# One ring of eight PSUM banks for all of a fused attention and feed-forward kernel, with its transposes spread

## Chip, cores and metric

One core of a Trainium2 chip. The metric is the device time of one execution in microseconds (us); every kernel that has a ratio ran beside runs of the kernel before on the same chip, and kernels of different calls (partly on different chips) are compared by these ratios. "TensorE" (PE in the profile) multiplies, "VectorE" (DVE) and "ScalarE" (ACT) read its results out of PSUM, "GpSimd" (POOL) casts and masks in SBUF, SP issues most transfers.

## The reference, cut to what matters

```python
# q, k, v: 8 batches x 8 heads x 576 x 64;  s: 8 x 8 x 576
scores = q @ k.T / 8 + min(-(cum_i - cum_j), 0)      # cum: running sum of max(s, 0)
attn = softmax(where(causal, -1e9, scores)) @ v
x = attn.transpose(0, 2, 1, 3).reshape(4608, 512)
out = (silu(x @ w_gate) * (x @ w_val)) @ w_out       # 512 -> 1536 -> 512
```

## The kernel before

Heads go one after the other. The first batch (8 heads) runs alone, since the feed-forward part needs its output; after that, feed-forward units of the tokens that are ready are laid between pieces of attention of the next batch. A unit is 4 matmuls of 512 columns into one PSUM bank: `pg` (gate), `pv` (value) or a third of `py` (output). k and q of a half-batch (4 heads) are transposed, by TensorE for half-batches 0 to 4, by transfers after that. Four extra rows per head in each of k and q (`aug`) carry the bias.

PSUM has 8 banks. They are shared out in three pools:

```python
scp = pool("scp", bufs=3, PSUM)    # scores
avp = pool("avp", bufs=1, PSUM)    # attn @ v
mp  = pool("mp",  bufs=4, PSUM)    # feed-forward, transposes of k and q (tps), of x (xps)
...
def score_piece(bh, ci):           # 4 pieces a head: 512, 512, 512 and 64 columns
    sc = scp.tile([128, 512], FP32, tag="sc")
    # ... one to four matmuls into sc ...
    nc.scalar.activation(pt[...], sc[:, 0:o], AF.Exp, scale=0.125)
    # pieces 0 and 3: GpSimd masks pt
...
def ffn_items(tt):
    for ft in range(12):
        pg = mp.tile(...)          # 4 matmuls
        # ACT: th = tanh(pg / 2);  DVE: pp = (th + 1) * pg
        yield
        pv = mp.tile(...)          # 4 matmuls
        # DVE: ht = pp * pv
        yield
    # ... 4 x py: 12 matmuls, ACT copies, SP stores ...
```

The transposes of half-batches 2 to 4 stand in one block right ahead of the scores that need them:

```python
if not first and step == 0 and 2 <= h < NPE:
    # ...
    cast_one(h, "k", nc.gpsimd); cast_one(h, "q", nc.gpsimd)
    for g in range(2):
        for nm in ("k", "q"):
            pe_transpose(h, nm, g)              # 5 or 4 transposes into one bank
            pe_out(h, nm, g, 0, nc.vector)      # copies partitions 0-63 out
            pe_out(h, nm, g, 1, nc.scalar)      # copies partitions 64-127 out
            yield ...
```

The softmax here doesn't subtract the row's maximum and nothing guards it: scores larger than these inputs give would overflow.

Of the kernel before, what the change touches and what calls it, by code (L numbers as in the profile page):

```python
# [15 lines left out]
ALU = mybir.AluOpType  # L16
# [3 lines left out]
def kernel(  # L20
# [32 lines left out]
    DIAG_OFF = [1088, 1216, 1344, 1472, 1024]  # L53
    OFF_OFF = {0: 0, 3: 448, 1: 512, 2: 832}
# [7 lines left out]
    CHUNK_PT = [1088, 0, 512, 1024]  # L62
# [15 lines left out]
    scp = ctx.enter_context(tc.tile_pool(name="scp", bufs=3, space=PSUM))  # L78
    avp = ctx.enter_context(tc.tile_pool(name="avp", bufs=1, space=PSUM))
    mp = ctx.enter_context(tc.tile_pool(name="mp", bufs=4, space=PSUM))  # L80
# [4 lines left out]
    NPE = 5  # L85
    KS = {i: dram.tile([NR * S, 128], BF16, name=f"ks{i}") for i in range(NPE, NHB)}
# [14 lines left out]
    HL = const.tile([BH, 4, 2, S], BF16)  # L101
    warm = const.tile([128, 1], FP32)

    with tc.manual_schedule():
        loaded = {}
        SRC = {"k": (k, 0), "q": (q, 1)}
# [31 lines left out]
        nc.sync.dma_start(s_sb, s.rearrange("b h n -> (b h) n"))  # L138
        load_qk(0)
        load_qk(1)  # L140
        load_v(0, range(5))

# [7 lines left out]
        nc.vector.memset(warm, 0.0)  # L150
        nc.scalar.activation(warm, warm, AF.Exp)
        nc.vector.memset(one_s, 1.0)
        nc.vector.memset(HL[:, 2:4, 0, :].bitcast(FP32), NEGS2)
        nc.vector.memset(HL[:, 0:2, 1, :].bitcast(FP32), ONES2)
        make_identity(nc, ident)
        for e in range(2):
            nc.gpsimd.memset(aug_rows(0, e)[:, 1, :], ONES2)
            nc.gpsimd.memset(aug_rows(0, e)[:, 0, :], 0.0)

            nc.scalar.copy(  # L160
                KQ[1][e][64 * (1 - e) : 64 * (1 - e) + 64, 1, :],
                one_s[:, 0:1].to_broadcast([64, NR * S + 64]),
            )
        nc.vector.memset(aug_rows(1, 0)[:, 0, :], 0.0)

        nc.vector.tensor_scalar(s_sb, s_sb, 0.0, 8.0, ALU.max, ALU.mult)
        nc.vector.tensor_tensor_scan(c8, one_s, s_sb, 0.0, ALU.mult, ALU.add)  # L167
        nc.vector.tensor_copy(HL[:, 0, 0, :], c8)
        nc.vector.tensor_sub(HL[:, 1, 0, :], c8, HL[:, 0, 0, :])
        nc.vector.tensor_copy(HL[:, 2:4, 1, :], HL[:, 0:2, 0, :])  # L170
        for r in range(2):
            for i in range(2):
                nc.vector.memset(KQ[i][r][64 * r : 64 * r + 64, :, NR * S :], 0.0)

        def aug(hb, engs):
            for hh in range(HB):
                r, e = divmod(hh, 2)
                r0 = 64 * (1 - r)
                engs[hh].dma_start(
                    KQ[hb % 2][r][r0 : r0 + 4, :, e * S : (e + 1) * S],  # L180
                    HL[hb * HB + hh : hb * HB + hh + 1, :, :, :],
                )

# [36 lines left out]
        def pe_transpose(hb, name, g):  # L220
            j0, j1 = JG[g]
            ps = mp.tile([128, j1 - j0, 128], BF16, tag="m", name="tps")
# [5 lines left out]
            tps[name, g] = ps  # L228

        def pe_out(hb, name, g, r, eng):  # L230
# [5 lines left out]
            srcp = tps[name, g][64 * r : 64 * r + 64].rearrange("a j x -> a x j")  # L236
            if eng is nc.scalar:
                nc.scalar.copy(dst, srcp)
            else:
                eng.tensor_copy(dst, srcp)  # L240

# [15 lines left out]

        def score_piece(bh, ci):
            hb, hh = divmod(bh, HB)
            if ci == 0:  # L260
# [4 lines left out]
            sc = scp.tile([128, 512], FP32, tag="sc", name="sc")  # L265
            o = 0
            for (tj, lo, hi) in CHUNKS[ci]:
# [3 lines left out]
                    T[:, 0, e * S + 128 * tj : e * S + 128 * (tj + 1)],  # L271
                    T[:, 1, e * S + lo : e * S + hi],
# [300 lines left out]
```

## Time and profile before

| | before |
|---|---|
| time, median of 4 runs | 414.9 us (413.6 to 415.5) |
| span of the profiled run | 411.9 us |
| TensorE busy | 383.5 us, 93% |
| TensorE busy from 100 to 300 us | 200.0 of 200 us |
| first feed-forward unit starts at | 36.3 us |

A profile line of a group has start or total, duration, engine, source line, operation, output, inputs and count; a bracket gives the idle time of the engine just before and what ended it. In a line of waits the waiting engine and line stand left of the arrow, the one waited for right of it, then total us, times and longest us. In a table of stages, the stretch comes first, then its length and the busy time of PE, PE's weight loads, DVE, ACT and POOL (instructions in brackets), TensorE's granted clock, the share of the DMA engines' time that was busy, and GB/s.

### The profile page before, as it was taken

What the parts mean: (1) busy time and instruction counts of PE and PEld (TensorE: products, weight loads), DVE (VectorE), ACT (ScalarE), POOL (GpSimd) and SP (SyncE); (2) the same over time, 40 slices, a digit from 0 to 9 for tenths busy, and PEclk for the clock granted to TensorE, in tenths of its full rate; (3) what the DMA queues carried; (4) which work ended last, traced back from release to release, by engine and by line L of the source; (5) the groups of instructions that cost most, each with busy time, mean ns of one, the idle gap of its engine ahead of it and who ended that gap; (6) DMA issues with size and microseconds to landing.
All of it is one profiled execution on the core that took longest, in us unless ns stands there. A gap on an engine that the chain in (4) does not pass through costs nothing.

```text
span 411.9 us, 7992 instructions
## 1 busy us (share of the span) xinstructions
PE 383.5 (93%) x3082; PEld 211.9 (51%) x3082; DVE 251.0 (61%) x494; ACT 212.0 (51%) x421; POOL 125.2 (30%) x224
## 2 busy tenths in 40 slices
PE   2687797989999999999999999999999999999996
PEld 1464454645555555555555555555555544444442
DVE  7846666366873588358844884479446733752750
ACT  7463665666555555456545564565556532322321
POOL 4783252743262316131623162316211110000000
PEclk9989998999999999999999999999999999999999
DMA  7999998466845793469346924681410002002002
GB/s 265 146 230 221 268 245 266 122 193 164 210 109 173 179 228 94 148 199 245 81 132 207 260 81 108 216 175 51 116 57 2 2 27 76 0 10 95 0 4 100
DMA packets 85335, 56.71 MB, mean 138 GB/s; under 512 B 65552, under 2 KB 69584, under 8 KB 85296
## 3 DMA queue, kind: packets, MB, share of 16 engines
q1 hardware_dynamic: 81360, 51.40, 44.8%
q0 software_dynamic: 3936, 4.79, 6.9%
q8 instruction: 24, 0.39, 0.4%
q14 instruction: 15, 0.12, 0.1%
HBM read 37.90 MB, written 15.93 MB: 131 GB/s over the span
## 4 chain that ended last, share of the span: by engine, by line
PE 90%; DVE 4%; DMA 2%; ACT 1%; POOL 1%; issue 1%; ACTq 0%; POOLq 0%
PE pg L457 23%; PE py L481 23%; PE pv L470 22%; PE sc L269 11%; PE av L305 7%; PE xps L337 3%; DVE kq L240 2%; DMA kq<-HL 1%; ACT pt L277 1%; DMA s_sb<-in_s_dram 1%; POOL vt L136 1%; PE tps L225 1%; DVE ot L321 1%; DVE c L167 0%; PE avm L305 0%
## 5 line engine op out<-in xcount | busy, mean ns | idle before, releaser
L277 ACT ACTIVATE pt<-sc 128x512 bf16<-128x512 f32 (+1 forms) x256 | 117.7, 505 | 56.2 <-PE sc L269 54.8
L464 DVE SCALAR_TENSOR_TENSOR pp<-th,pg 128x512 bf16<-128x512 bf16 x108 | 74.1, 686 | 63.8 <-ACT th L462 63.4
L457 PE MATMUL pg<-xt,wg 128*128 128x512 bf16 x432 | 111.8, 381 | 0.0
L470 PE MATMUL pv<-xt,wv 128*128 128x512 bf16 x432 | 110.9, 379 | 0.0
L462 ACT ACTIVATE th<-pg 128x512 bf16<-128x512 f32 x108 | 64.5, 597 | 86.0 <-PE pg L457 86.0
L481 PE MATMUL py<-wo,ht 128*128 128x512 bf16 x432 | 105.7, 379 | 0.0
L269 PE MATMUL sc<-kq 128*128 128x128 bf16 (+4 forms) x576 | 76.4, 247 | 10.4 <-DVE kq L240 5.5
L281 POOL TENSOR_SCALAR_AFFINE_SELECT pt<-pt 128x512 bf16<-128x512 bf16 x64 | 40.8, 637 | 140.0 <-ACT pt L277 137.7
L475 DVE TENSOR_TENSOR ht<-pp,pv 128x512 bf16<-128x512 bf16 x108 | 73.9, 684 | 7.9
L269 PEld LDWEIGHTS <-kq 128*128 128x128 bf16 x576 | 46.9, 101 | 44.3 <-issue 7.0
L457 PEld LDWEIGHTS <-wg 128*128 128x128 bf16 x432 | 38.5, 98 | 36.3 <-issue 0.8
L470 PEld LDWEIGHTS <-wv 128*128 128x128 bf16 x432 | 38.4, 98 | 34.8
L481 PEld LDWEIGHTS <-ht 128*128 128x128 bf16 x432 | 38.2, 98 | 34.9
L305 PEld LDWEIGHTS <-pt 128*128 128x128 bf16 x960 | 41.2, 98 | 20.9 <-issue 3.0
L305 PE MATMUL av<-vt,pt 128*128 128x65 bf16 x900 | 47.4, 194 | 2.0 <-POOL vt L136 0.9
L489 ACT ACTIVATE ysb<-py 128x512 f32<-128x512 f32 x36 | 21.5, 598 | 43.6 <-PE py L481 42.4
L286 POOL TENSOR_SCALAR_AFFINE_SELECT pt<-pt 128x64 bf16<-128x64 bf16 x64 | 15.4, 240 | 64.5 <-ACT pt L277 64.4
L341 DVE COPY xt<-xps 128x64 bf16<-128x64 bf16 (+7 forms) x32 | 9.7, 304 | 34.7 <-PE xps L337 34.7
L321 DVE TENSOR_TENSOR ot<-av,rc 128x320 bf16<-128x320 f32 x60 | 29.5, 491 | 2.1
L320 DVE RECIPROCAL rc<-av 128x5 f32<-128x5 f32 x60 | 11.4, 189 | 31.3 <-PE av L305 31.2
L136 POOL CAST vt<-rawv 128x512 bf16<-128x512 f32 (+1 forms) x40 | 25.7, 673 | 0.0
L240 DVE COPY kq<-tps 64x640 bf16<-64x640 bf16 (+1 forms) x24 | 17.5, 762 | 2.3 <-PE tps L225 2.1
(47 smaller groups left out, 160.6 us busy)
## 6 DMA issues: line engine op xcount, KB each, us to landing
rawk<-in_k_dram SPq DMA_DIRECT2D x16, 576.0 KB
rawq<-in_q_dram SPq DMA_DIRECT2D x16, 576.0 KB
out_dram<-ysb SPq DMA_DIRECT2D x36, 256.0 KB
rawv<-in_v_dram SPq DMA_DIRECT2D x32, 256.0 KB
ks<-ck SPq DMA_DIRECT2D x11, 288.0 KB
qs<-cq SPq DMA_DIRECT2D x11, 288.0 KB
wg<-in_moe_w_gate_dram POOLq DMA_DIRECT2D x2, 768.0 KB, 8.8
wv<-in_moe_w_val_dram POOLq DMA_DIRECT2D x2, 768.0 KB, 10.1
```

Of the source, the lines that this page charges most:

```text
L136: eng.tensor_copy(VT[b % 2][0:n, c, :, 0:D], loaded["v", b][0:n, c, :, :])
L269: nc.tensor.matmul(sc[:, o : o + w], T[:, 0, e * S + 128 * tj : e * S + 128 * (tj + 1)], T[:, 1, e * S + lo : e * S + hi], start=True, sto ...
L277: nc.scalar.activation(pt[:, CHUNK_PT[ci] : CHUNK_PT[ci] + o], sc[:, 0:o], AF.Exp, scale=0.125)
L281: nc.gpsimd.affine_select(pt[:, 1088:1600], pt[:, 1088:1600], pattern=[[0, 4], [1, 128]], compare_op=ALU.is_ge, fill=zreg, base=0, channel ...
L305: nc.tensor.matmul(av[:, bi * (D + 1) : (bi + 1) * (D + 1)], pt[:, c0 : c0 + 128], VT[b % 2][:, tj, h, :], start=(tj == 0), stop=(tj == bi),)
L321: nc.vector.tensor_mul(ot[:, :, e * D : (e + 1) * D], av3[:, :, 0:D], rc[:, :, None].to_broadcast([128, NCH, D]),)
L457: nc.tensor.matmul(pg, WG[j][:, c, f0 : f0 + 128], xt[:, c, :], start=(c == 0), stop=(c == 3),)
L462: nc.scalar.activation(th, pg, AF.Tanh, scale=0.5)
L464: nc.vector.scalar_tensor_tensor(pp, in0=th, scalar=1.0, in1=pg, op0=ALU.add, op1=ALU.mult)
L470: nc.tensor.matmul(pv, WV[j][:, c, f0 : f0 + 128], xt[:, c, :], start=(c == 0), stop=(c == 3),)
L475: nc.vector.tensor_mul(ht, pp, pv)
L481: nc.tensor.matmul(py, hts[ft][:, ts_ * 128 : (ts_ + 1) * 128], WO[ft // WKO][:, ft % WKO, :], start=(ft == 0), stop=(ft == NFT - 1),)
```

## The change

The intent: any bank may serve any use, and the bank that was given back longest ago is taken next; in the first batch one exp reads two banks at once, so a head needs two exps in place of four; and the transposes of half-batches 2 to 4 go one quarter at a time between feed-forward units, well ahead of their scores. The prologue is reordered too (fewer VectorE memsets, gate and value weights requested earlier and output weights one head later, two of the five v loads and the v casts later). Cut to the core:

```diff
-    scp = ...bufs=3 / avp = ...bufs=1 / mp = ...bufs=4
+    psp = ctx.enter_context(tc.tile_pool(name="psp", bufs=1, space=PSUM))
+    bank = [psp.tile([128, 2, 512], FP32, name=f"bank{i}") for i in range(4)]
+        def take(n=1):
+            if n == 1:
+                b = min(range(8), key=lambda i: released[i])
+                bs = [b]
+            else:                                   # a pair: both banks of one tile
+                b = 2 * min(range(4), key=lambda i: max(released[2 * i], released[2 * i + 1]))
+                bs = [b, b + 1]
+        def view(bs, w):
+            t = bank[bs[0] // 2].rearrange("p a n -> p (a n)")
+            o = 512 * (bs[0] % 2)
+            return t[:, o : o + w]
 def score_piece(bh, ci):
+            pair = WIDE or bh < H                   # WIDE = False: the first batch only
-            nc.scalar.activation(pt[...512...], sc[:, 0:o], AF.Exp, scale=0.125)
+                    c0, W = ((576, 1024), (0, 576))[ci // 2] if pair else ...
+                nc.scalar.activation(pt[:, c0 : c0 + W], sc[:, 0:W], AF.Exp, scale=0.125)
 def attn_items():
-                if not first and step == 0 and 2 <= h < NPE: ... all transposes of h
+                ahead = not first and 2 <= h and h + 1 < NPE
+                if ahead and step == 0: ... cast k and q of h + 1
+                        if ahead and ci == 1 and step: prep_one(h + 1, step - 1)
+                        if ahead and ci == 3 and step == 3: prep_one(h + 1, 3)
 hook = {
+            1: cast k and q of half-batch 2, 3 to 6: its four quarters, between units
```

More of the change, by code (lines that the diff above doesn't have):

```diff
@@ L51 @@
     NWCH = DF // WCH
-    DIAG_OFF = [1088, 1216, 1344, 1472, 1024]
-    OFF_OFF = {0: 0, 3: 448, 1: 512, 2: 832}
+    DIAG_OFF = [1088, 1216, 1344, 1472, 512]
+    OFF_OFF = {0: 576, 3: 1024, 1: 0, 2: 320}
     PTW = 1600
@@ L61 @@
     ]
-    CHUNK_PT = [1088, 0, 512, 1024]
+    CHUNK_PT = [1088, 576, 0, 512]
     def pt_col(tj, bi):
@@ L77 @@
     yp = ctx.enter_context(tc.tile_pool(name="yp", bufs=3))
-    scp = ctx.enter_context(tc.tile_pool(name="scp", bufs=3, space=PSUM))
-    avp = ctx.enter_context(tc.tile_pool(name="avp", bufs=1, space=PSUM))
-    mp = ctx.enter_context(tc.tile_pool(name="mp", bufs=4, space=PSUM))
+    psp = ctx.enter_context(tc.tile_pool(name="psp", bufs=1, space=PSUM))
     dram = ctx.enter_context(
@@ L85 @@
     NPE = 5
+    WIDE = False
     KS = {i: dram.tile([NR * S, 128], BF16, name=f"ks{i}") for i in range(NPE, NHB)}
@@ L105, with give, view16 @@
         loaded = {}
-        SRC = {"k": (k, 0), "q": (q, 1)}
+        SRC = {"q": (q, 0), "k": (k, 1)}
+        released = list(range(-8, 0))
+        clock = [0]
+        def take(n=1):
[5 more added lines that the diff above has]
+                bs = [b, b + 1]
+            assert max(released[i] for i in bs) < 1 << 40
+            for i in bs:
+                released[i] = 1 << 50
+            return bs
+        def give(bs):
+            clock[0] += 1
+            for i in bs:
+                released[i] = clock[0]
+        def view(bs, w):
+            t = bank[bs[0] // 2].rearrange("p a n -> p (a n)")
+            o = 512 * (bs[0] % 2)
+            return t[:, o : o + w]
+        def view16(bs, w):
+            t = bank[bs[0] // 2].rearrange("p a n -> p (a n)")
+            o = 512 * (bs[0] % 2)
+            return t[:, o : o + w // 2].bitcast(BF16)
         def load_one(hb, name, rs=(0, NR)):
@@ L136, in cast_v @@
             eng.tensor_copy(VT[b % 2][0:n, c, :, 0:D], loaded["v", b][0:n, c, :, :])
-        nc.sync.dma_start(s_sb, s.rearrange("b h n -> (b h) n"))
-        load_qk(0)
-        load_qk(1)
-        load_v(0, range(5))
         ONES2 = 1.0019378662109375
@@ L148, in aug_rows @@
             return KQ[i][r][r0 : r0 + 64, :, :].bitcast(FP32)
-        nc.vector.memset(warm, 0.0)
-        nc.scalar.activation(warm, warm, AF.Exp)
-        nc.vector.memset(one_s, 1.0)
-        nc.vector.memset(HL[:, 2:4, 0, :].bitcast(FP32), NEGS2)
-        nc.vector.memset(HL[:, 0:2, 1, :].bitcast(FP32), ONES2)
-        make_identity(nc, ident)
-        for e in range(2):
-            nc.gpsimd.memset(aug_rows(0, e)[:, 1, :], ONES2)
-            nc.gpsimd.memset(aug_rows(0, e)[:, 0, :], 0.0)
-            nc.scalar.copy(
-                KQ[1][e][64 * (1 - e) : 64 * (1 - e) + 64, 1, :],
-                one_s[:, 0:1].to_broadcast([64, NR * S + 64]),
-            )
-        nc.vector.memset(aug_rows(1, 0)[:, 0, :], 0.0)
-        nc.vector.tensor_scalar(s_sb, s_sb, 0.0, 8.0, ALU.max, ALU.mult)
-        nc.vector.tensor_tensor_scan(c8, one_s, s_sb, 0.0, ALU.mult, ALU.add)
-        nc.vector.tensor_copy(HL[:, 0, 0, :], c8)
-        nc.vector.tensor_sub(HL[:, 1, 0, :], c8, HL[:, 0, 0, :])
-        nc.vector.tensor_copy(HL[:, 2:4, 1, :], HL[:, 0:2, 0, :])
-        for r in range(2):
-            for i in range(2):
-                nc.vector.memset(KQ[i][r][64 * r : 64 * r + 64, :, NR * S :], 0.0)
         def aug(hb, engs):
@@ L178, in aug @@
                 r0 = 64 * (1 - r)
+                bh = hb * HB + hh
                 engs[hh].dma_start(
                     KQ[hb % 2][r][r0 : r0 + 4, :, e * S : (e + 1) * S],
-                    HL[hb * HB + hh : hb * HB + hh + 1, :, :, :],
+                    HL[bh : bh + 1, :, :, :],
                 )
+        nc.sync.dma_start(s_sb, s.rearrange("b h n -> (b h) n"))
+        load_qk(0)
+        load_qk(1)
+        load_v(0, range(3))
+        nc.vector.memset(warm, 0.0)
+        nc.scalar.activation(warm, warm, AF.Exp)
+        nc.vector.memset(one_s, 1.0)
+        nc.vector.memset(HL[:, 0:2, 0, :].bitcast(FP32), ONES2)
+        nc.vector.memset(HL[:, 2:4, 1, :].bitcast(FP32), NEGS2)
+        make_identity(nc, ident)
+        for r in range(2):
+            nc.gpsimd.memset(aug_rows(0, r), 0.0)
+            nc.scalar.mul(
+                KQ[1][r][64 * (1 - r) : 64 * (1 - r) + 64, 0, :],
+                one_s[:, 0:1].to_broadcast([64, NR * S + 64]), 0.0,
+            )
+        for r in range(2):
+            nc.gpsimd.memset(aug_rows(1, r)[:, 1, :], 0.0)
+            for i in range(2):
+                nc.gpsimd.memset(KQ[i][r][64 * r : 64 * r + 64, :, NR * S :], 0.0)
+        nc.vector.tensor_scalar(s_sb, s_sb, 0.0, 8.0, ALU.max, ALU.mult)
+        nc.vector.tensor_tensor_scan(c8, one_s, s_sb, 0.0, ALU.mult, ALU.add)
+        nc.vector.tensor_copy(HL[:, 0, 1, :], c8)
+        nc.vector.tensor_sub(HL[:, 1, 1, :], c8, HL[:, 0, 1, :])
+        nc.vector.tensor_copy(HL[:, 2:4, 0, :], HL[:, 0:2, 1, :])
         SP4 = [nc.sync] * 4
@@ L221, in pe_transpose @@
             j0, j1 = JG[g]
-            ps = mp.tile([128, j1 - j0, 128], BF16, tag="m", name="tps")
+            bs = take()
+            ps = view16(bs, (j1 - j0) * 128).rearrange("p (j x) -> p j x", x=128)
             ct = cts[name, hb]
@@ L227, in pe_transpose @@
                 )
-            tps[name, g] = ps
+            tps[name, g] = [ps, bs, 2]
         def pe_out(hb, name, g, r, eng):
@@ L235, in pe_out @@
             )[:, :, j0:j1]
-            srcp = tps[name, g][64 * r : 64 * r + 64].rearrange("a j x -> a x j")
+            tp = tps[name, g]
+            srcp = tp[0][64 * r : 64 * r + 64].rearrange("a j x -> a x j")
             if eng is nc.scalar:
@@ L240, in pe_out @@
                 eng.tensor_copy(dst, srcp)
+            tp[2] -= 1
+            if tp[2] == 0:
+                give(tp[1])
         def w_load(kind, j):
@@ L256 @@
         xts = {}
+        scs = {}
         def score_piece(bh, ci):
             hb, hh = divmod(bh, HB)
+            pair = WIDE or bh < H
             if ci == 0:
@@ L264, in score_piece @@
             T = KQ[hb % 2][r]
-            sc = scp.tile([128, 512], FP32, tag="sc", name="sc")
-            o = 0
+            if pair:
+                if ci % 2 == 0:
+                    bs = take(2)
+                    scs[bh] = bs
+                else:
+                    bs = scs[bh]
+                base = (512, 0, 0, 512)[ci]
+            else:
+                bs = take()
+                base = 0
+            o = base
+            n = sum(hi - lo for _, lo, hi in CHUNKS[ci])
+            sc = view(bs, 1024 if pair else 512)
             for (tj, lo, hi) in CHUNKS[ci]:
@@ L270, in score_piece @@
                     sc[:, o : o + w],
-                    T[:, 0, e * S + 128 * tj : e * S + 128 * (tj + 1)],
-                    T[:, 1, e * S + lo : e * S + hi],
+                    T[:, 1, e * S + 128 * tj : e * S + 128 * (tj + 1)],
+                    T[:, 0, e * S + lo : e * S + hi],
                     start=True,
@@ L276, in score_piece @@
                 o += w
-            nc.scalar.activation(
-                pt[:, CHUNK_PT[ci] : CHUNK_PT[ci] + o], sc[:, 0:o], AF.Exp, scale=0.125
-            )
-            if ci == 0:
+            if not pair or ci % 2 == 1:
+                if pair:
+                    c0, W = ((576, 1024), (0, 576))[ci // 2]
+                else:
+                    c0, W = CHUNK_PT[ci], n
+                nc.scalar.activation(pt[:, c0 : c0 + W], sc[:, 0:W], AF.Exp, scale=0.125)
+                give(bs)
+            if ci == (1 if pair else 0):
                 nc.gpsimd.affine_select(
@@ L286, in score_piece @@
                 nc.gpsimd.affine_select(
-                    pt[:, 1024:1088], pt[:, 1024:1088], pattern=[[1, 64]],
+                    pt[:, 512:576], pt[:, 512:576], pattern=[[1, 64]],
                     compare_op=ALU.is_ge, fill=zreg, base=0, channel_multiplier=-1,
@@ L295, in av_piece @@
             if bis[0] == 0:
-                if b == 0 and h % 2 == 1:
-                    avs[bh] = mp.tile([128, NCH * (D + 1)], FP32, tag="m", name="avm")
-                else:
-                    avs[bh] = avp.tile([128, NCH * (D + 1)], FP32, tag="av", name="av")
-            av = avs[bh]
+                bs = take()
+                avs[bh] = (view(bs, NCH * (D + 1)), bs)
+            av = avs[bh][0]
             pt = pts[bh]
@@ L317, in av_out @@
             ot = ots[pr]
-            av3 = avs.pop(bh).rearrange("p (c e) -> p c e", e=D + 1)
+            av, bs = avs.pop(bh)
+            av3 = av.rearrange("p (c e) -> p c e", e=D + 1)
             rc = small.tile([128, NCH], FP32, tag="rc", name="rc")
@@ L325, in av_out @@
             )
+            give(bs)
             pts.pop(bh)
@@ L333, in x_pe @@
                     xts[tt] = xtp.tile([128, 4, TT], BF16, tag="xt", name="xt")
-            ps = mp.tile([128, S], BF16, tag="m", name="xps")
+            bs = take()
+            ps = view16(bs, S)
             for c in range(NCH):
@@ L342, in x_pe @@
             nc.vector.tensor_copy(xts[b][:, r, TT - n0 : TT], ps[:, 0:n0])
-        wlate = {
-            0: ("g", 0), 1: ("v", 0), 3: ("g", 1), 5: ("v", 1), 7: ("o", 0), 8: ("o", 1),
-        }
+            give(bs)
+        wlate = {2: ("g", 1), 4: ("v", 1), 8: ("o", 0), 9: ("o", 1)}
         def side(h, step):
@@ L352, in side @@
             if h == 0:
-                if step == 0:
-                    for g in range(2):
-                        for nm in ("k", "q"):
-                            pe_transpose(1, nm, g)
-                            pe_out(1, nm, g, 0, nc.vector)
-                            pe_out(1, nm, g, 1, nc.vector)
-                if step == 1:
+                if step == 1:
+                    for r in range(2):
+                        for g in range(2):
+                            for nm in ("k", "q"):
+                                if r == 0:
+                                    pe_transpose(1, nm, g)
+                                prep1.append((nm, g, r))
+                    for nm, g, r in prep1[:4]:
+                        pe_out(1, nm, g, r, nc.vector)
+                if step == 2:
                     for c in range(5):
                         cast_v(0, c, nc.gpsimd)
+                    for nm, g, r in prep1[4:6]:
+                        pe_out(1, nm, g, r, nc.vector)
+                if step == 3:
+                    for nm, g, r in prep1[6:8]:
+                        pe_out(1, nm, g, r, nc.vector)
                 return
@@ L367, in side @@
                     load_qk(2)
+                if step == 3:
+                    pass
                 return
@@ L403, in side, with prep_one @@
                         cast_v(bn, 4, nc.gpsimd)
+        prep1 = []
+        def prep_one(hb, i):
+            g, nm = divmod(i, 2)
+            nm = ("k", "q")[nm]
+            pe_transpose(hb, nm, g)
+            pe_out(hb, nm, g, 0, nc.vector)
+            pe_out(hb, nm, g, 1, nc.scalar)
         def attn_items():
@@ L411, in attn_items @@
                 h, step = divmod(bh, HB)
-                if not first and step == 0 and 2 <= h < NPE:
-                    if h > 3:
-                        aug(h, SP4)
-                    cast_one(h, "k", nc.gpsimd)
-                    cast_one(h, "q", nc.gpsimd)
-                    yield kk + 0.01
-                    yield kk + 0.02
-                    for g in range(2):
-                        for nm in ("k", "q"):
-                            pe_transpose(h, nm, g)
-                            pe_out(h, nm, g, 0, nc.vector)
-                            pe_out(h, nm, g, 1, nc.scalar)
-                            yield kk + 0.03 + 0.02 * g
+                ahead = not first and 2 <= h and h + 1 < NPE
+                if ahead and step == 0:
+                    if h + 1 > 3:
+                        aug(h + 1, SP4)
+                    cast_one(h + 1, "k", nc.gpsimd)
+                    cast_one(h + 1, "q", nc.gpsimd)
                 if first and bh == H:
@@ L435, in attn_items @@
                         yield kk + 0.1 + ci / 8
+                        if ahead and ci == 1 and step:
+                            prep_one(h + 1, step - 1)
+                            yield kk + 0.1 + ci / 8
+                        if ahead and ci == 3 and step == 3:
+                            prep_one(h + 1, 3)
+                            yield kk + 0.1 + ci / 8
                 x = bh - lag - 1
@@ L454, in ffn_items @@
                 j, f0 = divmod(ft * 128, WCH)
-                pg = mp.tile([128, TT], FP32, tag="m", name="pg")
+                gbs = take()
+                pg = view(gbs, TT)
                 for c in range(4):
@@ L466, in ffn_items @@
                 )
+                give(gbs)
                 yield 1
-                pv = mp.tile([128, TT], FP32, tag="m", name="pv")
+                vbs = take()
+                pv = view(vbs, TT)
                 for c in range(4):
@@ L475, in ffn_items @@
                 nc.vector.tensor_mul(ht, pp, pv)
+                give(vbs)
                 hts.append(ht)
@@ L478, in ffn_items @@
             for ts_ in range(4):
-                py = mp.tile([128, DM], FP32, tag="m", name="py")
+                ybs = take()
+                py = view(ybs, DM)
                 for ft in range(NFT):
@@ L489, in ffn_items @@
                 nc.scalar.mul(ysb, py, 0.5)
+                give(ybs)
                 nc.sync.dma_start(
@@ L499 @@
         cast_one(0, "k", nc.scalar)
-        nc.vector.memset(aug_rows(1, 1)[:, 0, :], 0.0)
         cast_one(0, "q", nc.vector)
         aug(0, [nc.gpsimd] * 4)
-        for nm, eng in (("k", nc.scalar), ("q", nc.vector)):
+        w_load("g", 0)
+        aug(1, SP4)
+        load_v(0, (3, 4))
+        for nm in ("k", "q"):
             for g in range(2):
                 pe_transpose(0, nm, g)
-                pe_out(0, nm, g, 0, eng)
-        for nm, eng in (("k", nc.scalar), ("q", nc.vector)):
-            for g in range(2):
-                pe_out(0, nm, g, 1, eng)
+        for r in range(2):
+            for nm, eng in (("k", nc.scalar), ("q", nc.vector)):
+                for g in range(2):
+                    pe_out(0, nm, g, r, eng)
         init_vt(0)
-        aug(1, [nc.gpsimd] * 4)
         cast_one(1, "k", nc.vector)
         cast_one(1, "q", nc.vector)
+        w_load("v", 0)
         at = attn_items()
@@ L528 @@
         hook = {
+            1: [lambda: cast_one(2, "k", nc.gpsimd), lambda: cast_one(2, "q", nc.vector)],
+            3: [lambda: prep_one(2, 0)],
+            4: [lambda: prep_one(2, 1)],
+            5: [lambda: prep_one(2, 2)],
+            6: [lambda: prep_one(2, 3)],
             21: [lambda: load_qk(5)],
@@ L534 @@
             span = 36
-            n0 = 6 if tt == 0 else 0
+            n0 = 7 if tt == 0 else 0
             n = 0
```

## The prediction

> **What bounds the kernel now.** I read the page's busy shares and its 40 slices first, then busy time by stage, then TensorE's waits, then its timeline around the longest of them. From the page, the busy shares, then two rows of the slices (a slice is 10.3 us):
>
> ```profile
> PE 383.5 (93%) x3082; PEld 211.9 (51%) x3082; DVE 251.0 (61%) x494; ACT 212.0 (51%) x421; POOL 125.2 (30%) x224
> ...
> PE   2687797989999999999999999999999999999996
> ...
> PEclk9989998999999999999999999999999999999999
> ```
>
> From slice 10 on TensorE is full: its windows 103 to 200 us and 200 to 300 us are 97.00 and 100.00 us busy, and a feed-forward unit of 4 matmuls starts every 0.86 us. Nothing is to be won there by better buffers. What can be won lies in 411.9 - 383.5 = 28.4 us of idle PE, nearly all in slices 1 to 9, and in cold-clock matmuls behind the holes. Busy time by 6 us stage (engines in the page's order, then granted clock, DMA share, GB/s):
>
> ```profile
> 42.00:48.00 6.00, 3.30 (x32) 2.16 (x31) 4.92 (x8) 3.14 (x5) 0.00 (x0) 1.00 1.10 226
> ...
> 60.00:66.00 6.00, 3.88 (x45) 2.37 (x42) 5.01 (x11) 2.47 (x5) 2.43 (x3) 1.00 0.99 243
> 66.00:72.00 6.00, 5.27 (x40) 3.00 (x41) 2.34 (x6) 4.21 (x9) 0.88 (x2) 0.72 0.70 266
> ...
> 84.00:90.00 6.00, 4.12 (x46) 2.78 (x45) 3.70 (x7) 4.59 (x8) 1.38 (x2) 1.00 0.58 179
> ```
>
> Three holes stand among full stages, and after the second the clock is 0.72. TensorE's waits by what ended them (total, times, longest, us):
>
> ```profile
> PE tps L225 <- ACT ck L192: 6.7, 1, 6.7
> PE sc L269 <- DVE kq L240: 5.5, 3, 2.3
> PE sc L269 <- DMA kq<-HL: 3.3, 1, 3.3
> ...
> PE av L305 <- DVE ot L321: 0.9, 1, 0.9
> ```
>
> The first and third are the prologue. The second is the holes: scores of half-batches 2, 3 and 4 wait until VectorE has copied the transposed k and q out of PSUM. The second hole in TensorE's timeline (start, duration):
>
> ```profile
> 62.38 0.44 PE L225 MATMUL tps<-ident,ck 128*128 128x128 bf16 x5
> 63.17 0.45 PE L225 MATMUL tps<-ident,cq 128*128 128x128 bf16 x5 [0.35 <-POOL cq L194]
> 63.46 0.39 PE L225 MATMUL tps<-ident,ck 128*128 128x128 bf16 x4
> 64.04 0.38 PE L225 MATMUL tps<-ident,cq 128*128 128x128 bf16 x4 [0.19 <-DVE ht L475]
> 66.73 1.03 PE L269 MATMUL sc<-kq 128*128 128x128 bf16 x6 [2.30 <-DVE kq L240]
> 67.57 1.90 PE L457 MATMUL pg<-xt,wg 128*128 128x512 bf16 x4
> ```
>
> All 18 transposes are issued at once and the scores follow directly, so four 0.7 to 0.8 us copies are exposed. The unit at 67.57 takes 1.90 us instead of 1.03 and the scores 1.03 instead of 0.60: 1.3 us of cold clock on top.
>
> **What the Trainium skill says.** "TensorE: Matmul & The Clock Gate", part 1, says that the array drops to half clock after an idle window of about 3.4 us and comes back after a busy one; this trace agrees at the second hole (clock 0.72), though holes one and three did not trip it. "ScalarE: Activation LUTs", What ACT_TABLE_LOAD costs: an ACTIVATE with immediates costs 186 ns + 0.833 ns per element, and back-to-back ones overlap by 93 ns. The trace agrees: 596 ns at 512 columns (612 by the page), and a head's four exps in 1.69 us (4 x 93 + 1600 x 0.833 = 1705 ns). "PSUM — Partial Sum Buffer", The four PSUM rules and bank collisions: a matmul writes one bank, and engines on different banks may run together; so an exp over two banks is legal where each score matmul stays in one. No run here shows yet what an exp over two banks costs.
>
> **The change part by part.**
> (a) Transposes of half-batches 3 and 4 now lie one quarter at a time inside the previous half-batch's heads, a feed-forward unit or more apart. Hole two runs from 62.38 to 66.73 = 4.35 us; 18 transposes at some 0.056 us apart are 1.0 us of it. Lost 3.35 + 1.3 cold = 4.6 us. Hole three, 84.00 to 87.38, loses 3.38 - 1.0 = 2.4. The copies only change place, and VectorE in the full stage 54 to 60 us is 4.54 of 6 us busy, so it has room. I count all 7.0 us as gained.
> (b) Half-batch 2 can only be spread over the first feed-forward units. In the changed program's order its transposes sit after units 3 to 6 and its scores after unit 8. VectorE then has, from 1.7 us after the first unit's start (its first operation in the old kernel), six feed-forward operations at 0.69, a q cast at 0.72, two copies at 0.82 and two at 0.71: 7.9 us, finished at 9.6. TensorE reaches the scores after 8 x 0.86 + 1.0 = 7.9. So a wait of 1.7 us remains, against 47.43 - 43.26 - 1.0 = 3.2 before: gained 1.5.
> (c) The ring ends the single buffer of av: the 0.9 us wait (at 337.57 us) goes. Program order shows that a bank comes back no sooner than some 2 us of TensorE work after its last writer; elsewhere there was no wait to remove.
> (d) First batch: 8 heads x 2 fewer exps x 93 ns = 1.5 us of ScalarE, an upper bound. The head pitch from 23.2 to 31.2 us, the fourth to the eighth head, is 2.0 us against 1.69 of exp, because TensorE, masks and ot copies take turns with it; deeper banks help this too. Working the chain through with the measured durations, I get 12.5 us from the fourth head's scores to the first unit instead of 36.32 - 22.59 = 13.7: gained 1.2. The v casts go one head later, behind the third head's mask and a weight issue (0.64 + 0.76 us), and av of the first head waits for them (19.67 to 22.51 us now): lost 0.3 net, as q's cast starts about 1 us earlier, with fewer VectorE memsets ahead of it. Net 0.9.
> (e) New waits: k and q of half-batch 3 are now cast by GpSimd before the first mask of half-batch 2, some 15 us earlier than the 60.88 of before, while their loads are issued only at 45.38 with DMA saturated. Weight issues move (o later, g and v earlier), which should bring those loads forward. I charge 1.0 us.
> Sum: 4.6 + 2.4 + 1.5 + 0.9 + 0.9 - 1.0 = 9.3, so 415.1 - 9.3 = 405.8 us.
>
> **Rivals.** *DMA becomes the wait:* half-batch 3 arrives late, GpSimd stands in a cast, and masks and av behind it stall. For it: DMA share is about 1 from 20 to 67 us. Against it: nothing waited on rawk after 5.5 us, and a weight load is out of the way. It would leave 409 to 411. *The ring couples everything:* feed-forward units wait for banks that exps free late. For it: pools of 3 and 4 kept the two streams apart. Against it: reuse distance of 2 us or more, and no busy ACT or DVE stage over 85%. A 0.1 us stall per head over 56 heads would cost 5.6 us: 411. *VectorE hole:* in (b) the wait could be as long as before: 407. *First batch shrinks more:* if two-bank exps take the pitch to 1.6 us and the bias rows land earlier because two v loads wait, 2 to 3 us more: 403.
>
> **Range and chances.** The holes (9 us) are the secure part, the prologue and DMA the uncertain one: 401.5 to 411. A 2% gain needs 406.8 or less, just above my figure, so faster 0.57, same 0.42, slower 0.01.
>
> **What would show it.** PE idle falls from 28 to about 20 us. No wait of sc on the kq copies over 0.5 us for half-batches 3 and 4, one of 1 to 2 us for half-batch 2, and no slice below 8 between slice 4 and the last. The clock stays at 1.0 from 60 to 75 us. The first unit starts at about 35.4 instead of 36.3. ACT has 16 fewer exps. I am wrong if waits on raw k or q loads, or of pg and pv on ACT or DVE, exceed 2 us in all, or if the first unit starts after 37.

## More of the kernel before

TensorE's stage between 100 and 300 us:

```profile
100.00:300.00 200.00, 200.00 (x1695) 111.57 (x1694) 131.48 (x271) 110.63 (x227) 68.72 (x119) 1.00 0.60 159
```

No hole in 200 us and 1695 matmuls: the number to keep.

## The result

The changed kernel takes **649.9 us** (median of 4 runs, 646.7 to 651.7) against 414.9 us: a ratio of 1.566, 95% interval 1.558 to 1.574. A ratio is the mean time of one kernel's fast runs over that of the other's in the same rounds, so not quite the ratio of the medians quoted. Executions over 1.5% slower than the fastest of the same kernel are left out of the means. All runs are fast ones, and the results are correct. From its page, busy shares, TensorE's row of the slices (now of 16.2 us each) and its clock:

```profile
PE 443.4 (68%) x3029; PEld 231.3 (36%) x3082; DVE 254.5 (39%) x489; ACT 218.4 (34%) x405; POOL 123.9 (19%) x223
...
PE   2675567676777665755676667776577666877877
...
PEclk9777859998999999999999888955989989999999
```

The work of DVE, ACT and POOL is within about 3% of the 251.0, 212.0 and 125.2 us of before; the span around it grew, by 237.7 us. Of these, 59.9 are longer busy time of TensorE (443.4 against 383.5 us, at a mean granted clock of 0.92 over the run), the rest is waiting. And the loss is not in a few holes: where the row before holds 9s, this one holds 5 to 8. The stage from 100 to 300 us, of the changed kernel:

```profile
100.00:300.00 200.00, 134.73 (x1034) 72.77 (x1051) 79.48 (x162) 73.99 (x146) 45.84 (x78) 0.97 0.43 118
```

Where 1695 matmuls passed without a hole, 1034 pass with 65 us of holes, in the very stage in which my prediction saw nothing to be won. TensorE's waits, of the changed kernel:

```profile
PE bank L355 <- DVE pp L535: 21.4, 15, 1.5
PE bank L317 <- DVE ht L548: 19.5, 21, 1.5
PE bank L528 <- DVE ht L548: 14.7, 15, 1.3
PE bank L317 <- DVE pp L535: 14.1, 11, 1.5
PE bank L543 <- DVE pp L535: 13.3, 11, 2.1
```

L355 is `av`, L317 the scores, L528 `pg`, L543 `pv`. `av` needs nothing that `pp` makes, and scores nothing that `ht` makes, so these can only be waits for a buffer. VectorE's own waits need more care:

```profile
DVE ht L548 <- PE bank L543: 69.3, 55, 4.3
...
DVE ht L548 <- PE bank L317: 14.8, 11, 3.2
```

`ht` reads what L543 wrote, so the first is honest. The second looks like a false wait for scores (L317), but is no evidence of one: the profile names the work that ended last, and at 149.43 us, for one, `ht` started when its own `pv` had just ended (149.34 by the modelled ends) and a score matmul beside it too (149.37). In the program as built every `ht` waits on TensorE for its own `pv` only. A single instance of TensorE's own waits decides what is going on. Its timeline:

```profile
151.82 0.44 PE L355 MATMUL bank<-vt,pt 128*128 128x65 bf16 x9 [1.41 <-DVE pp L535]
...
153.90 0.38 PE L317 MATMUL bank<-kq 128*128 128x128 bf16 x4 [0.78 <-DVE ht L548]
...
156.62 1.02 PE L543 MATMUL bank<-xt,wv 128*128 128x512 bf16 x4 [1.25 <-DVE pp L535]
```

The nine matmuls at 151.82 are the second part of an `av` whose first part was written 2.6 us earlier into the same bank; nobody had read that bank in between. So it cannot be its own bank that it waits for. The ring's rule gives the banks without any timing, by following `take` and `give` through the program:

| at, us | writes | its bank | waits for DVE or ACT reading | that bank |
|---|---|---|---|---|
| 151.82 | av, 2nd part | 3 | pg (`pp`) | 2 |
| 153.90 | scores, piece 0 | 0 | pv (`ht`) | 1 |
| 156.62 | pv | 5 | pg (`pp`) | 4 |
| 158.66 | pg | 3 | scores, piece 3 (exp) | 2 |
| 162.33 | av | 0 | xps (copy to `xt`) | 1 |

Five of five wait for the other bank of their own two-bank tile: 2 and 3, 0 and 1, 4 and 5. The working theory: what the recorded program keeps apart is the declared tile and not the bank, so each bank has a neighbour through which its users and the neighbour's wait for each other. In the table the writer of one bank waits for an instruction whose own input TensorE had finished shortly before. In the first row `pg` ended at about 150.4, tanh and `pp` ran until 151.77, and TensorE did nothing for 1.41 us.

### The profile page after: what moved, and what is told of

The parts are those of the page before. It is cut to its first block, busy times and chain, and to the rows that moved or that the text cites. A ratio compares the mean times of both kernels' runs of the same rounds, so it can differ in the third digit from the quotient of the medians.

```text
span 649.6 us, 7986 instructions
## 1 busy us (share of the span) xinstructions
PE 443.4 (68%) x3029; PEld 231.3 (36%) x3082; DVE 254.5 (39%) x489; ACT 218.4 (34%) x405; POOL 123.9 (19%) x223
## 5 line engine op out<-in xcount | busy, mean ns | idle before, releaser
L330 ACT ACTIVATE pt<-bank 128x512 bf16<-128x512 f32 (+1 forms) x240 | 120.5, 525 | 183.2 <-PE bank L317 176.0
L543 PE MATMUL bank<-xt,wv 128*128 128x512 bf16 x413 | 122.5, 418 | 27.9 <-DVE pp L535 13.3
L535 DVE SCALAR_TENSOR_TENSOR pp<-th,bank 128x512 bf16<-128x512 bf16 x108 | 74.3, 688 | 169.4 <-ACT th L533 169.3
L528 PE MATMUL bank<-xt,wg 128*128 128x512 bf16 x414 | 120.1, 410 | 29.5 <-DVE ht L548 14.7
L317 PE MATMUL bank<-kq 128*128 128x128 bf16 (+4 forms) x576 | 83.0, 258 | 70.3 <-DVE ht L548 19.5
L533 ACT ACTIVATE th<-bank 128x512 bf16<-128x512 f32 x108 | 64.5, 597 | 171.0 <-PE bank L528 165.4
L556 PE MATMUL bank<-wo,ht 128*128 128x512 bf16 x416 | 104.6, 382 | 15.0 <-ACT pt L330 7.0
L548 DVE TENSOR_TENSOR ht<-pp,bank 128x512 bf16<-128x512 bf16 x108 | 74.2, 687 | 88.0 <-PE bank L543 69.3
L317 PEld LDWEIGHTS <-kq 128*128 128x128 bf16 x576 | 51.4, 105 | 107.6 <-issue 81.2
L355 PE MATMUL bank<-vt,pt 128*128 128x65 bf16 x960 | 53.0, 201 | 42.4 <-DVE pp L535 21.4
L355 PEld LDWEIGHTS <-pt 128*128 128x128 bf16 x960 | 46.2, 103 | 69.0 <-issue 52.6
L543 PEld LDWEIGHTS <-wv 128*128 128x128 bf16 x432 | 42.3, 105 | 74.6 <-issue 45.1
L528 PEld LDWEIGHTS <-wg 128*128 128x128 bf16 x432 | 41.8, 103 | 75.2 <-issue 46.0
L564 ACT ACTIVATE ysb<-bank 128x512 f32<-128x512 f32 x36 | 21.5, 597 | 54.9 <-PE bank L556 51.6
L372 DVE TENSOR_TENSOR ot<-bank,rc 128x320 bf16<-128x320 f32 x64 | 31.5, 492 | 2.2
```

The costliest lines, as they stand in the source:

```text
L317: nc.tensor.matmul(sc[:, o : o + w], T[:, 1, e * S + 128 * tj : e * S + 128 * (tj + 1)], T[:, 0, e * S + lo : e * S + hi], start=True, sto ...
L330: nc.scalar.activation(pt[:, c0 : c0 + W], sc[:, 0:W], AF.Exp, scale=0.125)
L355: nc.tensor.matmul(av[:, bi * (D + 1) : (bi + 1) * (D + 1)], pt[:, c0 : c0 + 128], VT[b % 2][:, tj, h, :], start=(tj == 0), stop=(tj == bi),)
L372: nc.vector.tensor_mul(ot[:, :, e * D : (e + 1) * D], av3[:, :, 0:D], rc[:, :, None].to_broadcast([128, NCH, D]),)
L528: nc.tensor.matmul(pg, WG[j][:, c, f0 : f0 + 128], xt[:, c, :], start=(c == 0), stop=(c == 3),)
L533: nc.scalar.activation(th, pg, AF.Tanh, scale=0.5)
```

## Experiments

### Is it the tile? Three kernels

*Eight tiles of one bank* (an exp over two banks is then impossible):

```diff
-    bank = [psp.tile([128, 2, 512], FP32, name=f"bank{i}") for i in range(4)]
+    bank = [psp.tile([128, 512], FP32, name=f"bank{i}") for i in range(8)]
-            pair = WIDE or bh < H
+            pair = False
```

> The changed kernel with the same ring, but each of its 8 banks declared as a tile of its own, and one exp per bank in the first batch too (an exp over two banks is then impossible). Theory N (false waits between the two halves of a two-bank tile: what is recorded as touched is the whole tile, so a matmul into one bank waits for ACT or DVE reading the other): 403 to 413 us, and no wait of av on DVE pp or of sc on DVE ht above 2 us in all. Rival R (the order of the ring itself couples the streams: each bank comes back too early): 600 to 660 us, as nothing of the order of reuse changes after the first batch. Rival D (the 9.0 us in which GpSimd waited for raw k of half-batch 3, and its consequences): 640 us.

*Without pairs*, tiles of two banks kept (the second edit alone):

> The changed kernel with its four two-bank tiles, but exps over one bank in the first batch. Theory N: the tiles still span two banks, so 630 to 670 us. Rival P (exps over two banks cause it, directly or by what they leave behind in the ring): near 410 us. It also separates the two edits of the run with eight tiles.

*Two tiles of four banks*, no pairs:

```diff
-    bank = [psp.tile([128, 2, 512], ...) for i in range(4)]      # bank[b // 2], column 512 * (b % 2)
+    bank = [psp.tile([128, 4, 512], ...) for i in range(2)]      # bank[b // 4], column 512 * (b % 4)
```

> As the run without exps over two banks, but the ring's 8 banks lie in two tiles of four banks each. Theory N: each bank now has three neighbours whose readers it must wait for, so clearly slower than 650 us, 800 to 1000 us. Rival R and P: unchanged against the run with two-bank tiles, as banks, order of reuse and reuse distance are the same.

| banks in a tile | time | TensorE busy, 100 to 300 us |
|---|---|---|
| 1 | 412.4 us median of 4 (ratio to before 0.993, 0.989 to 0.997) | 200.0 us |
| 2 | 653.9 us, one run of unknown state | 139.8 us |
| 4 | 947.4 us, one run of unknown state | 128.1 us, clock 0.63 |

The stage from 100 to 300 us with one bank, with two, and with four, to a tile:

```profile
100.00:300.00 200.00, 200.00 (x1693) 111.56 (x1692) 131.47 (x270) 110.95 (x229) 68.51 (x119) 1.00 0.60 158
```

```profile
100.00:300.00 200.00, 139.78 (x1064) 74.00 (x1064) 79.48 (x163) 75.55 (x147) 46.31 (x78) 0.94 0.40 110
```

```profile
100.00:300.00 200.00, 128.10 (x665) 61.16 (x665) 49.10 (x99) 48.93 (x93) 28.20 (x49) 0.63 0.23 66
```

Busy time hides how bad the last is; the count of matmuls does not: 1693, 1064 and 665 in the same 200 us. The three kernels have the same ring rule, order, banks and exps; only the declaration differs. This settles the tile as the cause: the gaps are some 240 and 290 us, and the four runs with eight tiles lie within 3 us. It falls out that pairs are innocent (653.9 against 649.9) and that the ring's order is (412.4). In the run with eight tiles, no wait of av on `pp` or of scores on `ht` is left. The built programs say the same without a clock: of the 347 waits in the changed kernel's TensorE instructions for VectorE or ScalarE to be done with PSUM, 332 name an instruction that reads only the other bank of the tile; with eight tiles it is none of 545. I also built the kernel without pairs with the tile's bank index written out in place of the flattened view: its TensorE instructions wait for the same instructions in the same places, so it was not run. One trap: the two-bank program has fewer waits in all in its TensorE instructions than the eight-tile one (577 against 800). A wait costs by when its release comes, not by being there.

### What is left of the expected gain?

With the fault gone, 412.4 us is still 6.6 us short of my 405.8. Three parts were separated.

*The spread transposes alone*, on the old pools and prologue:

> The kernel before, with its pools and its prologue, and only the PE transposes of half-batches 2 to 4 placed as in the changed kernel. My prediction's parts (a) and (b) alone: 4.6 + 2.4 + 1.5 = 8.5 us of gain, less up to 1 for later loads: 406 to 409 us. Rival V (copies on VectorE and ScalarE crowd the feed-forward units and masks, and k and q of half-batch 3 come too late for the earlier casts): 412 us or more.

Measured: 413.6 us, ratio 0.995 (0.991 to 0.999). A gain of some 2 us in place of 8.5: rival V, whose second half stands in the trace (GpSimd waited 16.2 us for raw k).

*The ring alone* on the kernel before:

> The kernel before with nothing changed but the ring of 8 one-bank tiles in place of its three pools. If TensorE's steady stage has nothing to win and the single av buffer costs 0.9 us: 413.5 to 415 us, within 0.5% of the kernel before. If a shared ring lets streams wait for each other: 417 us or more.

Measured: 415.0 us, ratio 0.997 (0.992 to 1.002): no difference shown, as expected; the 0.9 us wait of av on `ot` is gone from its trace.

*Ring and spread with the old prologue*:

> The kernel before with its own prologue, plus the ring of 8 one-bank tiles, plus the spread transposes. If the 3 us by which the first feed-forward unit starts later in the run with eight tiles (39.4 against 36.3 us) come from the changed prologue (v casts one head later and the last two v loads behind the bias rows), it starts at 36.3 again and the whole takes 408 to 410 us. If they come from the ring in the first batch, it stays at 411 to 413.

Measured: 412.6 us, ratio 0.993 (0.988 to 0.997). The first unit starts at about 36 us again, against 39.5 with eight tiles and the changed prologue, so the prologue does cost some 3 us. TensorE's wait for v casts in the first batch, in the run with eight tiles:

```profile
PE bank L351 <- POOL vt L162: 5.1, 5, 2.2
```

But the total did not improve, against what I expected (408 to 410 us): something later took it back. The next two steps came from these traces.

*One reader a bank.* In the eight-tile run, the scores of half-batch 3 still wait 2.27 us although their transposes had been spread. Timeline of that moment:

```profile
66.44 0.72 ACT L265 COPY kq<-bank 64x512 bf16<-64x512 bf16 x1 [1.62 <-DVE kq L267]
67.68 0.59 ACT L529 ACTIVATE th<-bank 128x512 bf16<-128x512 f32 x1
68.30 0.69 DVE L531 SCALAR_TENSOR_TENSOR pp<-th,bank 128x512 bf16<-128x512 bf16 x1 [1.90 <-ACT th L529]
...
68.91 0.70 DVE L267 COPY kq<-bank 64x512 bf16<-64x512 bf16 x1
69.67 0.40 PE L313 MATMUL bank<-kq 128*128 128x128 bf16 x4 [2.27 <-DVE kq L267]
```

ScalarE's copy of partitions 64 to 127 waits for VectorE's copy of 0 to 63 of the same bank (1.62 us). tanh stands behind it in ScalarE's queue until 67.68, VectorE idles for 1.90 us until that tanh, its next copy comes after `pp`, at 68.91, and the scores after that copy. All told, in the run with ring, spread and old prologue:

```profile
ACT kq L265 <- DVE kq L267: 11.3, 11, 1.6
```

```diff
-            pe_out(hb, nm, g, 0, nc.vector)
-            pe_out(hb, nm, g, 1, nc.scalar)
+            eng = nc.vector if nm == "k" else nc.scalar
+            pe_out(hb, nm, g, 0, eng)
+            pe_out(hb, nm, g, 1, eng)
```

> As the run with ring, old prologue and spread transposes, but VectorE copies both halves of k and ScalarE both halves of q, so no bank of transposes is read by two engines; the number of copies of each engine is the same. Theory S (ScalarE stands in its copy until VectorE has finished reading the same bank, tanh queues behind it, and VectorE's next copy behind a pp that waits for that tanh): ScalarE's waits for VectorE's kq copies (7 to 8 us in all) vanish, the waits of scores for kq copies fall from 4.5 us to under 2.5, 2 to 3 us faster than that run. Rival L (the copies' load alone, 0.7 to 0.8 us each, is what the scores wait for): no change of time.

Measured: 410.9 us, ratio 0.987 (0.984 to 0.991) against 0.993. ScalarE's waits for VectorE's copies are gone, and those of the scores for kq copies fell from 7.2 to 3.3 us (I had said under 2.5). The gain is 1.7 us by the medians, where I had said 2 to 3. The intervals overlap, though each of the four runs was faster than each of the four with two readers, beside which they ran; the trace carries the cause. That two engines may not read one bank at once is what the Trainium skill's page "PSUM — Partial Sum Buffer" (PSUM bank collisions raise a hardware error) asks for, by bank and 32-partition quadrant. These two copies lie in different quadrants, which the page calls clean; this program separates them all the same, and no run here tried them together.

*Raw k and q come late.* Stages of the run with one reader a bank, and GpSimd's wait in it:

```profile
48.00:54.00 6.00, 2.35 (x17) 1.07 (x15) 3.05 (x6) 2.30 (x5) 2.31 (x3) 1.00 1.00 356
54.00:60.00 6.00, 3.47 (x24) 2.17 (x25) 1.56 (x4) 0.00 (x0) 5.15 (x10) 0.50 0.80 132
```

```profile
POOL ck L219 <- DMA rawk<-in_k_dram: 16.6, 1, 16.6
```

TensorE works 5.8 of these 12 us, the second half at clock 0.50. The change casts k and q of half-batch 3 ahead of half-batch 2's first mask; the data land at 51 us, and masks, v casts and `av` stand behind in GpSimd's queue. First remedy: cast after that head's masks and v casts.

```diff
-                if ahead and step == 0:   ... cast_one(h + 1, "k"), cast_one(h + 1, "q")
+                        if ahead and step == 0 and ci == 3:   # after the head's last mask
+                            ... cast_one(h + 1, "k"), cast_one(h + 1, "q")
```

> As the run with one reader a bank, but GpSimd casts k and q of half-batch 3 after the masks of the first head of half-batch 2 and the v casts, not before them. Theory K (the early casts stand 16 to 17 us on raw k, which lands at 51 us, and masks, v casts and av stand behind them: 48 to 60 us hold 5.8 us of TensorE work in 12): most of these 6 us come back, 404 to 408 us, with no wait of GpSimd on raw k above 3 us. Rival B (raw k of half-batch 3 and v of the batch land too late for anything placed there): 410 to 411 us, the wait moves to the transposes.

Measured: 411.3 us, median of the 5 fast runs of 6 (406.3 to 412.1; a sixth, 412.7, counts as slow), ratio 0.985 (0.979 to 0.992), not told apart from the run before it: a miss. The wait has moved, as rival B had it, to the transposes:

```profile
PE bank L251 <- POOL ck L219: 6.1, 1, 6.1
```

Second remedy, on top: the two output-weight loads are issued with heads 9 and 11 in place of 7 and 8, behind the loads of v, k and q.

```diff
-    wlate = {..., 7: ("o", 0), 8: ("o", 1)}
+    wlate = {..., 9: ("o", 0), 11: ("o", 1)}
```

> As the run with later casts, and the two loads of the output weights issued with heads 9 and 11 in place of 7 and 8, so that raw v, k and q land ahead of them. If DMA bandwidth is what delays raw k in the run with later casts: 1 to 2 us faster than it. If what is late there is no longer waited for: the same, within 0.3%.

Measured: **403.8 us**, median of 5 (403.1 to 404.5), ratio **0.971** (0.968 to 0.974). I had expected 1 to 2 us and got 7.5 by the medians, 6 by the ratios. The same stages in this run:

```profile
48.00:54.00 6.00, 5.79 (x49) 3.15 (x49) 4.87 (x8) 4.07 (x9) 5.78 (x10) 1.00 1.15 324
54.00:60.00 6.00, 5.95 (x62) 3.79 (x61) 4.44 (x10) 5.41 (x12) 2.28 (x4) 1.00 1.22 200
```

```profile
PE   2477999999999999999999999999999999999995
```

From the fifth slice to the last but one TensorE is at least 90% busy. The loads are the same, only their order changed: raw k of half-batch 3 is issued at 43.0 us, against 46.45 in the run with later casts, and GpSimd casts it at 49.9 without a wait, against 54.9 after a wait of 3.7 us.

### Controls

*Later output weights alone*, on the kernel before:

> The kernel before with nothing changed but the two loads of the output weights issued with heads 9 and 11 in place of 7 and 8. If the later weight loads help only where transposes are spread (they bring raw k of half-batch 3 forward, which the old placement does not need early): 414 to 417 us, within 0.5% of the kernel before. If they are worth something by themselves: 411 us or less.

Measured: 415.8 us, ratio 1.000 (0.993 to 1.008). No gain shows where nothing asks for k early.

*The fastest kernel on the old pools*:

> As the fastest run (spread transposes, one reader a bank, later casts, later output weights), but with the old kernel's three PSUM pools in place of the ring. If the ring is worth only the single av buffer's 0.9 us and the 1 us or so that feed-forward units waited for a free buffer while transposes held them: 404.5 to 406.5 us. If the ring is what lets the spread placement pay (transposes, feed-forward and xps share 4 buffers): 409 us or more.

Measured: 406.8 us, ratio 0.980 (0.973 to 0.986), just outside what I had said. So the ring adds up to 1% on top of the spread; these two ran on different chips, and I compare their ratios, whose intervals touch.

*Exps over two banks, with the fault kept out*: the whole changed kernel, but with two two-bank tiles for exps and four single ones during the first batch, then eight single ones.

> The changed kernel entire, but its ring declared in two steps: in the first batch two tiles of two banks for the exps over two banks and four of one bank for all else, and from the first feed-forward unit eight tiles of one bank. Theory N: the false waits go where they cost, so 408 to 413 us. Against the run with eight tiles (four exps a head in the first batch) it prices the exps over two banks: a head's exps take 1.56 us in the changed kernel against 1.69 before, 8 x 0.13 = 1.0 us at most, if ScalarE bounds the first batch; 0 if the masks, copies and v casts do.

Measured: 413.8 us, ratio 0.995 (0.991 to 0.999), against 0.993 for the run with eight tiles. No gain shows, and the time is just above the 408 to 413 us that I had said. ScalarE's timeline for one head, before and in the changed kernel:

```profile
25.46 1.69 ACT L277 ACTIVATE pt<-sc 128x512 bf16<-128x512 f32 x4 [0.53 <-PE sc L269]
```

```profile
29.36 1.57 ACT L330 ACTIVATE pt<-bank 128x1024 bf16<-128x1024 f32 x2 [0.61 <-PE bank L317]
```

0.12 us a head, 1.0 us for eight. That is less than the estimate of 2 x 93 = 186 ns which I had taken from the skill's page "ScalarE: Activation LUTs", and ScalarE is not what the first batch waits for longest: in the run with the fault kept out it waited 5.92 us for the scores that stood behind the late v casts.

## Why the prediction was wrong

The figure was 405.8 us in a range of 401.5 to 411; 649.9 came.

1. **The step that failed is part (c) and the rival built on it.** "Program order shows that a bank comes back no sooner than some 2 us of TensorE work after its last writer" holds for banks, but the unit of waiting is the tile, and the tile was declared with two. Counted along the built program at 0.86 us for a unit (an estimate), a bank comes back at least 1.9 us after its last writer once the first batch is over; of the two-bank tile, half of all uses begin within some 1.5 us of its last writer, a quarter within 0.2. I read `[128, 2, 512]` in the diff as a way to make the wide exp possible, and asked after the order of reuse, not after what shares a tile. The rival "the ring couples everything" named the symptom, two streams that wait for each other, with the wrong cause and the wrong size (0.1 us a head). Measured: 412.4 us with one bank to a tile, 653.9 with two, 947.4 with four. The prediction's own sign of being wrong came true: `pg` and `pv` waited far more than 2 us on ACT and DVE, 14.7 and 13.3 in the two largest groups alone.
2. **Steady stage, "nothing is to be won there by better buffers"**: right (ring alone 0.997), but from there being nothing to win I concluded that nothing could be lost.
3. **Part (a), 7.0 us**: the mechanism was right and it came in the end, once two conditions held that I had not checked: data there in time, and copies that do not wait for each other. As changed, half-batch 3's scores still waited 2.27 us (eight-tile run). The trace before had a hint that I passed over: ScalarE's copies had 9.0 us of idle time before them, 8.1 of it ended by VectorE's copies. (The cold clock was counted from the trace. But the idle stretch ahead of it was 2.30 us, shorter than the page's window, so "this trace agrees" holds only for the fall of the clock and its return.)
4. **Part (b), a remaining wait of 1.7 us**: 2.2 us in the eight-tile run. The size was near, but VectorE was not busy throughout, as I summed it; it idled for tanh behind ScalarE's waiting copy.
5. **Part (c)'s 0.9 us** of av on `ot`: gone, too little for the time to show.
6. **Part (d), the first unit 0.9 us earlier**: it started at 39.5 us, 3.2 later, in the eight-tile run. I charged the v casts 0.3 us for standing one head later; TensorE waited 5.1 us for them, in part because the last two v loads, now behind the bias rows, were late (GpSimd waited 1.9 us on raw v). The 1.5 us of ScalarE was 1.0, and bought no time that shows. (My check of the page's figures was also off: of four ACTIVATEs in a row three overlap, not four, which makes an estimate of 1798 ns and not 1705, against 1.69 us measured.)
7. **Part (e), 1.0 us for late k and q**: the rival "DMA becomes the wait" was right, and cost about 6 us of the 12 between 48 and 60 us in the run with one reader a bank. In the changed kernel itself GpSimd waited 9.0 us for raw k. I priced a queue that stops (masks, casts and `av` behind one cast) like a single delay.

What stays open: how much of the changed prologue's 3 us is the order of the casts and how much the late loads; and whether two engines may copy different quadrants of a bank at once here.

## What to carry to other kernels

When buffers are put together into one declared tile, ask who else lives in it: independent users of one tile wait for each other, and here that added 57% to the run time while VectorE's and ScalarE's instructions kept their length (`pp` 686 and 688 ns). In a trace the sign is a wait between two instructions that share neither data nor a bank, above all in the middle of an accumulation; first see that the instruction named is not merely the one that happened to end last. And before work is moved earlier, check that its inputs land earlier: spreading the transposes alone was worth 2 us, and with ring, one reader a bank and later casts the order of two weight loads still decided between 6 us and 12.

## What the Trainium skill lacked or had wrong

- "PSUM — Partial Sum Buffer" advises to guard PSUM by bank and quadrant. It does not say that a tile declared over several banks is waited for as a whole by a recorded program: 412.4, 653.9 and 947.4 us with one, two and four banks to a tile.
- The same page calls reads of different quadrants of one bank clean. The page doesn't say that such reads may be kept apart all the same: in the run with ring, spread and old prologue ScalarE waited 11.3 us in 11 cases for VectorE's copy of the other half of the partitions.
- "ScalarE: Activation LUTs", What ACT_TABLE_LOAD costs, has no word on an ACTIVATE that reads across two banks. It runs at the page's rate: 1025 ns at 1024 columns, where the estimate 186 + 0.833 x 1024 gives 1039. But two such instructions in a row saved 0.12 us over four, not 0.19.
- "TensorE: Matmul & The Clock Gate" puts the fall to half clock after an idle window of about 3.4 us. In the kernel before the clock fell (0.72 from 66 to 72 us) after an idle stretch of 2.30 us that followed two shorter ones; no run here shows how busy a window may be and still count as idle.
